# Depthwise and gate steps inside blocks of the second channel product; stores, weight jobs and first loads placed elsewhere

## The chip, the cores and the metric

One core of one Trainium2 chip runs the whole program. The metric is the device time of one execution in microseconds. The kernel before took 1010.52 us (median of 3 runs, 1009.43 to 1011.03).

## The reference, cut to what matters

Three stages follow each other, all in float32; batch B = 4, 12 heads of 64, sequence S = 448, model width 768.

```
attn = sigmoid(q @ k.T / 8 - log S) @ v          # 48 heads, no softmax
x    = attn, heads side by side                  # (4, 448, 768)
h    = (x.T @ U @ V).T ;  u = x + h              # token mixing, rank 32
y    = u + relu(u @ w_ch1) @ w_ch2               # 768 -> 3072 -> 768
gate = sigmoid(causal 5-tap depthwise conv of y over S)
out  = ((y @ w_val) * gate) @ w_out
```

## The kernel before, in words

Activations lie in SBUF transposed (128 channels on the partitions, 448 positions along the row) in one tile `xs`, 6 channel blocks for each of 4 batches. Every float32 product that must be exact is made of three matmuls: an operand is cut into a high part (a copy on ACT that rounds to fp32r) and a low part (a subtraction on DVE), and `mm3` (L438 to L440) adds high x high, high x low and low x high. The large products are also done in Strassen's way, with seven products instead of eight over two batches and two halves of the channels (`seven`, L795). TensorE (PE) therefore needs, for every pair of weight blocks, seven tiles of sums and differences of weights (A11, A12, S2, S1, S3, S4, A22), each with a high and a low half.

**Stages.** `attention_phase` (24 pairs of heads, two per round; the token mixing of batches 0 and 1 lies between its rounds), then `main_phase`: pass p = 0 over batches 0 and 1, pass p = 1 over batches 2 and 3. A pass has six quads q. A quad is two chains of the first channel product (`chain`, 7 x 9 matmuls each, with relu into `hs`) and four blocks of the second (`ch2`, L917: for each of two column halves and two batches 4 x 9 matmuls, then one DVE addition of three PSUM banks into `xs`, L936). So a quad has 270 matmuls in 30 groups of nine. After pass 1 come the value product, the gate and the output product.

**Order.** All engines run hand-placed programs in order. After nearly each group of nine matmuls the program calls `step()`, which takes the next weight job off one list (`pump`, L169), a second one after every eighth step of pass 0 and every fourth of pass 1, and none while the job would bring the live weight tiles over WS = 10. Small parts are put off with `deferred` to the next `flush()`, `later` to the one after. The list is written by `plan()` (L1120): for pass 0 each quad's weights are unpacked from float64 bits, kept in device memory (`keep`) and split; for pass 1 they are read back and split. Each quad of pass 1 lists `pair_jobs` of both chains (6 jobs each), `second_jobs` (4 jobs, or 8 plain loads in quad 0), 3 `gate_jobs` and 13 `form_jobs` for the later value and output weights. Float64 or read-back data come through three `raw` buffers: a load is issued when a buffer's reader is placed (`load_next`).

**Side work.** `sides` maps (pass, quad, event) to units: the token mixing of batches 2 and 3 in pass 0 (transposes, projection, and three `add` units of six small matmuls, L757, that use both banks of `ps_a`), and parked sums `u_sums`. Event 0 comes after the first chain of a quad, event 1 after the second, events 2 to 5 after the four blocks of `ch2`. The last group of a chain (A22, `tail`) is held back and runs after the first group of what follows. In the `ps_a` banks lie also a chain's `y` and `z`; DVE reads them in `both` (L863).

**Queues.** In `main_phase` all transfers are issued by SP in program order: raw loads (L163, L159), kept copies (L196), stash stores and loads (L332, L417), parked tiles (L611). An issue waits in its queue until its data or buffer is ready, and those behind it wait too. `x` tiles have XS = 6 buffers, and a buffer is free again when its kept copy has landed.

**First loads.** `load_kq` (L449) of pair 0: keys (`kq[:, 0]`, 128 rows) on SP, the two halves of the queries (`kq[.., 1]`) on ACT and POOL. `prep_pair` (L480) casts keys on DVE (L490) and queries on ACT (L501), then makes the low parts on DVE (L493), and `scores` (L515) starts.

Of the kernel before, what the change touches and what calls it, by code (L numbers as in the profile page):

```python
# [23 lines left out]
QUAD = 4  # L24
# [23 lines left out]
def tile_kernel(  # L48
# [18 lines left out]
    nc = tc.nc  # L67
# [4 lines left out]
    def later(part):  # L72
        deferred.append(lambda: deferred.append(part))
# [118 lines left out]
    def keep(slot, part, x):  # L192

        if slot not in kept:
            kept[slot] = pools["kept"].tile([P, 2, HQ], F32, tag="kept", name="k_%s%d" % slot)
        side_queue().dma_start(kept[slot][:, part], x)  # L196
# [83 lines left out]
    def second_jobs(p, q):  # L280

        out = []

        def fresh(n, half):
            def job():
                t = wtile(f"w2_{p}_{n}_{half}")
                x = to_x(("w2", n, half))

                def done():
                    forms[p, n, half] = t  # L290
                    keep((f"h{half}_", n // 2), n % 2, x)

                later(lambda: in_two(x, t, done))
            return job

        def again(n, half):
            def job():
                a = loaded.pop(("x", f"h{half}_", n // 2, p))
                ts = [wtile(f"w2_{p}_{n + i}_{half}") for i in range(2)]

                def done(i):
                    forms[p, n + i, half] = ts[i]
                    if i:
                        load_next()

                for i in range(2):
                    in_two(a[:, i], ts[i], lambda i=i: done(i))
            return job

        for half in range(2):  # L310
            kept_already = p or ("w2", QUAD * q, half) in ahead
            for n in range(QUAD * q, QUAD * q + QUAD, 2 if kept_already else 1):
                if kept_already:
                    out.append((2, again(n, half), ("x", f"h{half}_", n // 2, p)))
                else:
                    out.append((1, fresh(n, half), ("w2", n, half)))
        return out
# [131 lines left out]
    def load_kq(p):  # L449

        kq = pools["kq"].tile([P, 2, S], F32, tag="kq", name=f"kq{p}")
        if p == 0:
            nc.sync.dma_start(kq[:, 0], kq_in[p, :, 0])
            for h, queue in enumerate((nc.scalar, nc.gpsimd)):
                queue.dma_start(kq[D * h:D * h + D, 1], kq_in[p, D * h:D * h + D, 1 + h])
        else:
            nc.sync.dma_start(kq[:D], kq_in[p, :D, :2])
            nc.sync.dma_start(kq[D:], kq_in[p, D:, 0::2])
        return kq
# [454 lines left out]
            f"fin{p}_{k}", lambda ws: fetched["out", k, ws, src], f"z{p}", both, last_of, step, before  # L914
        )

    def ch2(p, q, b, half, step, before=None):  # L917
        three = trio(f"ch2_{p}_{q}_{b}_{half}")
        ps = [three[:, j, :S] for j in range(KH)]
        for i in range(QUAD):  # L920
            done_with()
            flush()
            w = weight(p, QUAD * q + i, half)
            if b == halves[p][-1]:
                spent.append(1)
            h = hs[p, QUAD * q + i, b]
            for j in range(KH):
                mm3(ps[j], w, j, h, i == 0, i == QUAD - 1)
            if i < QUAD - 1:
                step()  # L930
            if before and not i:
                before()

        def add():
            y = x_rows(b, half)
            nc.vector.tensor_add(y, three[:, :, :S], y)  # L936

        deferred.append(add)
        step()
# [88 lines left out]
    def attention_phase():  # L1028


        for p, kq in enumerate([load_kq(p) for p in range(2)]):
            load_v(p, kq)
        nc.vector.memset(bias, -math.log(S))
        warm = scratch("warm")[:, :1]
        nc.scalar.activation(warm, bias, AF.Sigmoid)
        nc.gpsimd.memset(xs[:, :, :, :PAD], 0.0)

        zeros = operand("zeros")
        nc.vector.memset(f32(zeros[:, 0]), 0.0)
        idle = pools["ps_s"].tile([P, 2, 512], F32, tag="sc", name="idle")  # L1040
        for _ in range(IDLE):
            mm(idle[:, 0, :S], zeros[:, 0, :P], zeros[:, 0], start=True, stop=True)
        prep_pair(0)
        load_pair(2)
        consts = load_mix()
        steps = prep_mix(*consts)
        side = {(0, 2): steps[:1], (1, 1): steps[1:2], (1, 2): steps[2:]}
        for b in halves[0]:
            units = mix_units(b)
            r = 3 * b + 3  # L1050
            for at, some in (
                ((r, 2), units[:2]),
                ((r + 1, 0), units[2:4]),
                ((r + 1, 2), units[4:5]),
                ((r + 2, 0), units[5:6]),
                ((r + 3, 0) if b == 0 else (r + 2, 2), units[6:]),
            ):
                side[at] = some
        rounds = NP // 2
        todo = [part for k in range(KH) for part in u_sums(0, k)]  # L1060
        def put(at, *parts):
            side[at] = side.get(at, []) + list(parts)

        put((0, 2), *[lambda: load_next(nc.sync)] * RAWS)
        at = iter([(q, k) for q in range(1, rounds) for k in range(3)][2:])
        for key in full_keys + part_keys:
            for part in ahead[key]:
                slot = next(at)
                side[slot] = [part] + side.get(slot, [])
        for slot, n in (((9, 0), 1), ((9, 1), 1), ((9, 2), 2), ((10, 0), 1), ((10, 1), 1), ((10, 2), 2), ((11, 0), 1)):  # L1070
            put(slot, *todo[:n])
            del todo[:n]
        for slot, n in (((10, 1), 1), ((10, 2), 1), ((11, 0), 1), ((11, 1), 2), ((11, 2), 2)):
            put(slot, *[pump] * n)

        def values(p):
            for c in range(NKC):
                attend(p, c)

        def between(q, k):  # L1080
            for step in side.get((q, k), ()):
                step()

        for q in range(rounds):
            p = 2 * q
            for c in range(NKC):
                scores(p, c)
            flush()
            last = q == rounds - 1
            if q:  # L1090
                values(p - 1)
                between(q, 0)
                attend_rest(q - 1)
            else:
                prep_pair(1)
            if not last:
                scores_rest(q)
            flush()
            load_pair(p + 3)
            load_pair(p + 4)  # L1100
            between(q, 1)
            prep_pair(p + 2)
            for c in range(NKC):
                scores(p + 1, c)
            flush()
            values(p)
            between(q, 2)
            prep_pair(p + 3)
        scores_rest(rounds - 1)
        flush()  # L1110
        pump()
        flush()
        values(NP - 1)
        attend_rest(rounds - 1)
# [5 lines left out]
    def plan():  # L1120
# [30 lines left out]
        more = [job for kind in ("val", "out") for k in range(KH) for job in form_jobs(kind, k)]  # L1151
        share = -(-len(more) // (NQ - 1))
        for q in range(NQ):
            for c in (QUAD * q, QUAD * q + 2):
                give(pair_jobs(1, c))
            give(second_jobs(1, q) if q else ready_jobs(1))
            jobs.extend(gate_jobs(halves[0], q))
            give(more[:share])
            del more[:share]

    def main_phase():
# [72 lines left out]
        for p, bs in enumerate(halves):  # L1234
            often[0] = 4 if p else 8
            for q in range(NQ):
                last = q == NQ - 1
                events = iter(range(6))

                def side():  # L1240
                    for unit in sides.pop((p, q, next(events)), ()):
                        unit()

                for i in range(2):
                    if last and i:
                        renew("y" if p else 1)
                    tail = chain(p, QUAD * q + 2 * i, step, tail if i else None)
                    side()
                for half in range(2):
                    for b in bs:  # L1250
                        if last and p and half and b == bs[0]:
                            open_late()
                        ch2(p, q, b, half, step, tail)
                        tail = None
                        if last and p:
                            fetch_next((2, 4, 0, 4)[2 * half + b - bs[0]])
                        side()
                while last and rush:
                    step()
                    flush()  # L1260
# [186 lines left out]
```

## Time and profile before

| | us |
|---|---|
| median of 3 runs | 1010.52 |
| lowest, highest | 1009.43, 1011.03 |
| the profiled execution | 1006.96 |
| its span, first to last instruction | 1005.2 |
| mean granted TensorE clock, share of full | 0.995 |

| engine | busy us | share |
|---|---|---|
| PE matmul | 989.5 | 98% |
| PE weight load | 840.2 | 84% |
| DVE | 736.3 | 73% |
| ACT | 465.5 | 46% |
| POOL | 21.7 | 2% |

Matmuls overlap in the array: one of 448 columns is shown as about 0.37 us, and the next starts about 0.2 us after it. A busy PE therefore says little by itself; the starts of its matmuls and the idle time in brackets say where it stood. In the rows below a line of a timeline is start, duration, engine, line, operation and tiles, and how many like it follow each other (x); the bracket is the idle time of the engine before it, and what ended it.

### The profile page before, as it was taken

The page shows a single profiled execution, that of the slowest core. Times are in us where ns is not written, and L with a number is a line of the kernel's source. Part 1 is how long each engine was busy: PE and PEld are TensorE (multiplying, and loading weights), DVE is VectorE, ACT ScalarE, POOL GpSimd, SP SyncE. Part 2 cuts the span into 40 slices and gives each one's busy share as a digit, 9 for nine tenths or more (in the row PEclk, how much of TensorE's full clock was granted, in tenths as well). Part 3 has the DMA queues.
Part 4 walks back from the last instruction along what each step waited for, and adds up shares of the span by engine and source line. Part 5 has one row for each costly group of instructions (what it writes and reads, how often), then busy time and mean ns, then how long its engine had stood idle before and what let it go on. Part 6 is the DMA issues. An engine that isn't in the chain of part 4 may idle for free.

```text
span 1005.2 us, 14580 instructions
## 1 busy us (share of the span) xinstructions
PE 989.5 (98%) x5208; PEld 840.2 (84%) x5208; DVE 736.3 (73%) x1324; ACT 465.5 (46%) x871; POOL 21.7 (2%) x40
## 2 busy tenths in 40 slices
PE   8999999999999999999999999999999999999998
PEld 4555448988887999998999999998999999999997
DVE  4767797656677787878747979788879777993631
ACT  5767685344353363636333545536354433431331
POOL 0111110000000000000000000000000000000000
PEclk9999999999998999999999999999999999999999
DMA  6967666534546575774835657364546276833745
GB/s 177 273 191 199 164 152 204 169 93 132 141 110 197 172 223 170 221 220 151 313 118 185 221 172 253 118 257 147 210 155 207 98 294 230 282 125 122 258 149 189
DMA packets 83001, 187.52 MB, mean 187 GB/s; under 512 B 14992, under 2 KB 34640, under 8 KB 82928
## 3 DMA queue, kind: packets, MB, share of 16 engines
q1 hardware_dynamic: 79824, 174.64, 55.5%
q0 software_dynamic: 2880, 11.72, 3.9%
q8 instruction: 41, 0.67, 0.3%
q14 instruction: 32, 0.26, 0.1%
q10 hardware_dynamic: 224, 0.23, 0.1%
HBM read 129.14 MB, written 57.41 MB: 186 GB/s over the span
## 4 chain that ended last, share of the span: by engine, by line
PE 62%; DVE 4%; DMA 2%; ACT 1%; issue 1%; SPq 0%; DVEq 0%; ACTq 0%
PE ch L438 9%; PE ch L439 9%; PE ch L440 9%; PE x L438 4%; PE x L440 4%; PE x L439 4%; PE z L438 2%; PE z L440 2%; PE z L439 2%; PE val L439 1%; PE x_fin L439 1%; PE x_fin L440 1%; PE x_fin L438 1%; PE val L440 1%; PE val L438 1%; PE y L438 1%
## 5 line engine op out<-in xcount | busy, mean ns | idle before, releaser
L438 PE MATMUL ch<-h,w 128*128 128x448 f32 x576 | 212.4, 369 | 0.0
L439 PE MATMUL ch<-h,w 128*128 128x448 f32 x576 | 211.7, 368 | 0.2 <-DVE h L858 0.2
L440 PE MATMUL ch<-h,w 128*128 128x448 f32 x576 | 211.5, 367 | 0.0
L438 PEld LDWEIGHTS ch<-h,w 128*128 128x128 f32 x576 | 108.5, 188 | 11.4 <-issue 2.1
L439 PEld LDWEIGHTS ch<-h,w 128*128 128x128 f32 x576 | 108.6, 189 | 10.0 <-DVE h L858 0.8
L440 PEld LDWEIGHTS ch<-h,w 128*128 128x128 f32 x576 | 108.6, 189 | 9.4
L936 DVE TENSOR_TENSOR xs<-ch,xs 128x1344 f32<-128x1344 f32 x48 | 74.7, 1556 | 55.1 <-PE ch L440 55.0
L510 ACT ACTIVATE a<-sc,bias 128x896 f32<-128x896 f32 x72 | 67.3, 1007 | 9.7 <-PE sc L522 9.7
L104 DVE SCALAR_TENSOR_TENSOR x_w<-x_w,r_w 128x384 uint32<-128x384 uint32 x84 | 46.9, 559 | 31.1 <-ACT x_w L100 24.7
L553 PE MATMUL av<-a,vr 128*64 128x448 f32 x288 | 59.4, 548 | 1.3 <-DVE xs L575 1.3
L522 PEld LDWEIGHTS sc<-ks 64*128 64x128 f32 x432 | 38.3, 186 | 23.8 <-ACT a L510 5.1
L522 PE MATMUL sc<-ks 64*128 64x448 f32 x432 | 53.2, 384 | 2.6 <-ACT ks L501 1.2
L100 ACT ACTIVATE x_w<-raw_w 128x384 f32<-128x384 f32 x84 | 45.4, 546 | 19.0 <-DMA k_h<-x_w 8.4
L440 PE MATMUL x<-T,S 128*128 128x448 f32 x144 | 52.9, 368 | 0.5 <-DVE S L203 0.5
L439 PE MATMUL x<-T,S 128*128 128x448 f32 x144 | 52.7, 366 | 0.0
L438 PE MATMUL x<-T,S 128*128 128x448 f32 x144 | 52.7, 366 | 0.0
L553 PEld LDWEIGHTS av<-a,vr 128*64 128x64 f32 x288 | 18.5, 136 | 31.4 <-issue 27.4
L200 ACT ACTIVATE S<-raw_x_w 128x384 fp32r<-128x384 f32 x48 | 23.2, 518 | 38.8 <-DVE raw_x_w L252 12.2
L857 ACT ACTIVATE h<-x 128x448 fp32r<-128x448 f32 x24 | 13.1, 544 | 42.8 <-PE x L440 42.8
L857 ACT ACTIVATE h<-p 128x448 fp32r<-128x448 f32 x48 | 27.5, 573 | 11.3 <-DVE p L863 11.3
L200 ACT ACTIVATE A<-x_w 128x384 fp32r<-128x384 f32 x36 | 18.6, 523 | 27.6 <-PE ch L440 21.9
L200 ACT ACTIVATE S<-x_w 128x384 fp32r<-128x384 f32 x48 | 23.2, 517 | 16.5 <-DVE x_w L260 6.3
(304 smaller groups left out, 2177.5 us busy)
## 6 DMA issues: line engine op xcount, KB each, us to landing
raw_w<-in_w SPq DMA_DIRECT2D x79, 384.0 KB, 3.5
kq<-in_kq SPq DMA_DIRECT2D x47, 224.0 KB, 4.6
raw_x_w<-k_w SPq DMA_DIRECT2D x24, 384.0 KB, 4.5
k_w<-x_w SPq DMA_DIRECT2D x43, 192.0 KB, 3.8
f_val_A<-s_val_A SPq DMA_DIRECT2D x21, 384.0 KB, 3.8
f_out_S<-s_out_S SPq DMA_DIRECT2D x20, 384.0 KB, 3.3
k_h<-x_w SPq DMA_DIRECT2D x36, 192.0 KB, 3.8
raw_w<-in_w POOLq DMA_DIRECT2D x17, 384.0 KB, 4.4
```

The lines of the kernel that those rows point to most:

```text
L100: nc.scalar.activation(f32(x), f32(high), AF.Prelu, scale=2.0 ** -112, alpha=-(2.0 ** 32))
L104: nc.vector.scalar_tensor_tensor(x, x, 3, r, op0=ALU.logical_shift_left, op1=ALU.bitwise_or)
L200: nc.scalar.activation(t[:, 0], x, AF.Copy)
L438: mm(ps, wk[:, 0], x[:, 0], start=start, stop=False, **kw)
L439: mm(ps, wk[:, 0], x[:, 1], start=False, stop=False, **kw)
L440: mm(ps, wk[:, 1], x[:, 0], start=False, stop=stop, **kw)
L510: nc.scalar.activation(a[:, :, :], ps[:, :, :S], AF.Sigmoid, bias=bias, scale=1.0 / math.sqrt(D))
L522: mm(ps[:, h, :S].rearrange("p (c s) -> p c s", c=NSC), ks[r, tk, 0, c], ks[r, tq, 1, :, :SC], start=t == 0, stop=t == 2,)
L553: mm(att["ps"][D * h:D * h + D, :S], vr[:, h, c], a[:, h], start=c == 0, stop=False,)
L857: nc.scalar.activation(t[:, 0], x, AF.Relu)
L936: nc.vector.tensor_add(y, three[:, :, :S], y)
```

## The change

Five edits; the computation stays the same:

1. `second_jobs`: the kept copy of a freshly unpacked block of `w2` is put off by one flush only, instead of being issued with the block's low part two flushes further on.
2. `load_kq`, pair 0: SP and ACT each load one half of the rows, queries first and then keys; POOL issues none.
3. `ch2` has a new argument `inside`, called after its second group of nine matmuls and the step that follows it. `main_phase` passes `side`, so events 1 to 4 lie inside the four blocks of `ch2`; event 0 stays after the first chain, event 5 after the last block. None is left after the second chain.
4. Last round of the attention: `attend_rest` before `between(q, 0)` instead of after it.
5. `plan`, pass 1: the second chain's six jobs and the `second_jobs` are one list `a`; gate and form jobs (16 in quads 0 to 4, 3 in quad 5) are dealt out evenly behind its jobs, instead of all following them.

```diff
-                    keep((f"h{half}_", n // 2), n % 2, x)
-
+
+                deferred.append(lambda: keep((f"h{half}_", n // 2), n % 2, x))
                 later(lambda: in_two(x, t, done))
...
         if p == 0:
-            nc.sync.dma_start(kq[:, 0], kq_in[p, :, 0])
-            for h, queue in enumerate((nc.scalar, nc.gpsimd)):
-                queue.dma_start(kq[D * h:D * h + D, 1], kq_in[p, D * h:D * h + D, 1 + h])
+            for h, queue in enumerate((nc.sync, nc.scalar)):
+                r = slice(D * h, D * h + D)
+                queue.dma_start(kq[r, 1], kq_in[p, r, 1 + h])
+                queue.dma_start(kq[r, 0], kq_in[p, r, 0])
...
             if before and not i:
                 before()
+            if inside and i == 1:
+                inside()
...
                 values(p - 1)
+                if last:
+                    attend_rest(q - 1)
                 between(q, 0)
-                attend_rest(q - 1)
+                if not last:
+                    attend_rest(q - 1)
...
-            for c in (QUAD * q, QUAD * q + 2):
-                give(pair_jobs(1, c))
-            give(second_jobs(1, q) if q else ready_jobs(1))
-            jobs.extend(gate_jobs(halves[0], q))
-            give(more[:share])
+            give(pair_jobs(1, QUAD * q))
+            a = pair_jobs(1, QUAD * q + 2) + (second_jobs(1, q) if q else ready_jobs(1))
+            rest = [(*job, None) for job in gate_jobs(halves[0], q)] + more[:share]
+            n = len(a)
+            for i, job in enumerate(a):
+                give([job] + rest[i * len(rest) // n:(i + 1) * len(rest) // n])
             del more[:share]
...
                     tail = chain(p, QUAD * q + 2 * i, step, tail if i else None)
-                    side()
+                    if not i:
+                        side()
...
-                        ch2(p, q, b, half, step, tail)
+                        ch2(p, q, b, half, step, tail, side)
...
-                        side()
+                side()
```

## Rows read from the trace of the kernel before

**Rows 1.** The page's first part: busy time, share and instructions of each engine.
```profile
PE 989.5 (98%) x5208; PEld 840.2 (84%) x5208; DVE 736.3 (73%) x1324; ACT 465.5 (46%) x871; POOL 21.7 (2%) x40
```

**Rows 2.** Waits of PE: line, releaser, us in total, times, longest.
```profile
PE h L757 <- DVE u L863: 3.2, 2, 2.2
PE x L438 <- DVE p L863: 1.7, 2, 1.1
```

**Rows 3.** Timeline of PE around three `add` units of the mixing.
```profile
238.26 0.46 PE L757 MATMUL h<-vst,pst 32*128 32x448 f32 x1
239.73 0.88 PE L757 MATMUL h<-vst,pst 32*128 32x448 f32 x5 [1.00 <-DVE u L863]
...
303.19 0.47 PE L757 MATMUL h<-vst,pst 32*128 32x448 f32 x1
305.86 1.48 PE L757 MATMUL h<-vst,pst 32*128 32x448 f32 x5 [2.20 <-DVE u L863]
307.27 0.74 PE L438 MATMUL ch<-h,w 128*128 128x448 f32 x1
...
311.92 0.51 PE L438 MATMUL x<-T,A 128*128 128x448 f32 x1
...
318.85 0.87 PE L757 MATMUL h<-vst,pst 32*128 32x448 f32 x6
```

**Rows 4.** Windows: length, busy (count) PE, PEld, DVE, ACT, POOL; PEclk; DMA, GB/s.
```profile
305.40:312.20 6.80, 6.34 (x18) 5.23 (x19) 4.22 (x9) 0.98 (x2) 0.00 (x0) 0.50 0.77 258
```

**Rows 5.** The same view of three stretches of 100 us and one of 204 us.
```profile
350.00:450.00 100.00, 100.00 (x495) 92.67 (x494) 85.12 (x164) 49.41 (x103) 0.00 (x0) 1.00 0.70 208
490.00:590.00 100.00, 100.00 (x485) 90.85 (x484) 68.38 (x116) 40.03 (x80) 0.00 (x0) 1.00 0.55 187
484.50:688.50 204.00, 204.00 (x988) 185.31 (x988) 159.04 (x268) 85.26 (x173) 0.00 (x0) 1.00 0.58 201
700.00:800.00 100.00, 100.00 (x495) 92.63 (x494) 83.23 (x140) 44.63 (x91) 0.00 (x0) 1.00 0.51 172
```

**Rows 6.** Timeline of the first 10 us.
```profile
0.74 0.55 ACTq L455 DMA_DIRECT2D kq<-in_kq  x1
...
1.25 0.65 POOL L455 DMA_DIRECT2D kq<-in_kq  x1 [0.80 <-POOLq L1436]
...
3.58 0.40 DVE L490 CAST ks<-kq 128x448 fp32r<-128x448 f32 x1 [2.22 <-DMA kq<-in_kq]
...
5.67 0.58 ACT L501 ACTIVATE ks<-kq 128x448 fp32r<-128x448 f32 x1 [2.85 <-DMA kq<-in_kq]
...
7.61 2.31 PE L522 MATMUL sc<-ks 64*128 64x448 f32 x14 [0.18 <-DVE ks L506]
```

**Rows 7.** DMA issues of pair 0 on ACT's queue: count, size, us to landing.
```profile
kq<-in_kq ACTq DMA_DIRECT2D x1, 112.0 KB, 3.2
```

**Rows 8.** Timeline at the end of the attention, PE and DVE.
```profile
145.72 2.48 PE L553 MATMUL av<-a,vr 128*64 128x448 f32 x12 [1.27 <-DVE xs L575]
...
153.79 1.15 DVE L575 COPY xs<-av 128x448 f32<-128x448 f32 x2
...
157.46 0.47 PE L440 MATMUL x<-T,S 128*128 128x448 f32 x1 [0.50 <-DVE S L203]
```

**Rows 9.** Timeline of ACT near the end of pass 0.
```profile
463.85 0.55 ACT L100 ACTIVATE x_w<-raw_w 128x384 f32<-128x384 f32 x1 [3.52 <-DMA k_h<-x_w]
```

**Rows 10.** Timeline of DVE in pass 1, quad 3.
```profile
687.54 0.56 DVE L251 TENSOR_TENSOR raw_x_w<-raw_x_w 128x384 f32<-128x384 f32 x1 [2.75 <-DMA raw_x_w<-k_w]
```

**Rows 11.** DMA issues of read-back weights: count, size, median us to landing.
```profile
raw_x_w<-k_w SPq DMA_DIRECT2D x24, 384.0 KB, 4.5
w<-s_w SPq DMA_DIRECT2D x16, 384.0 KB, 4.3
```

**Rows 12.** Costliest groups: one split's high copy on ACT, low part on DVE.
```profile
L203 DVE TENSOR_TENSOR S<-raw_x_w,S 128x384 fp32r<-128x384 f32 x48 | 24.8, 553 | 3.5 <-ACT S L200 3.4
L200 ACT ACTIVATE S<-raw_x_w 128x384 fp32r<-128x384 f32 x48 | 23.2, 518 | 38.8 <-DVE raw_x_w L252 12.2 <-issue 10.4 <-DVE raw_x_w L260 7.1
```

More of the change, by code (lines that the diff above doesn't have):

```diff
@@ L915, in fin_chain, with ch2 @@
         )
-    def ch2(p, q, b, half, step, before=None):
+    def ch2(p, q, b, half, step, before=None, inside=None):
         three = trio(f"ch2_{p}_{q}_{b}_{half}")
```

## The prediction

> **What bounds the kernel now.** I read the engine totals first: PE is busy for 989.5 of 1005.2 us, DVE for 736.3, ACT for 465.5 [rows 1]. The reader is to see there that PE sets the end, and that there is at most some 16 us of idle time to win, plus what lies hidden in slow matmuls. Then the list of PE's waits [rows 2]: in the whole main phase few are over half a microsecond, and four are named by two lines, the mixing's `add` units waiting for DVE (3.2 us in two) and the chains' A22 group waiting for DVE's `p` (1.7 us in two). Then PE's timeline at these places [rows 3], the granted clock there [rows 4], and the count of matmuls in equal stretches [rows 5]. The last shows something that no list of waits shows: with PE never idle and the clock granted in full, 495 matmuls fit into 100 us at 350 and at 700 us, but 485 at 490 us. PE runs at one of two spacings, 202 or 206 ns. The change must therefore be judged by four things: stalls of PE, the clock, the spacing, and new stalls.
>
> **The change part by part.** Times are for the profiled execution, 1006.96 us, which is 3.56 us under the median of the runs; I carry the sum over to the median unchanged.
>
> *Mixing units inside `ch2`.* Before, the `add` unit of event 1 stands right behind the second chain, whose `z` DVE has still to read from the bank that the unit needs. Two of them stall: the first small matmul to the second takes 239.73 - 238.26 = 1.47 us and 305.86 - 303.19 = 2.67 us, while an undisturbed unit issues six in a row [rows 3]. That is 4.1 us. After the second stall the granted clock is half (1.2 instead of 2.4 GHz) until 312.2 us [rows 4]: five small matmuls take 1.48 instead of 0.88 us (0.6 us), and the 12 intervals from 307.27 to 311.92 us take 4.65 instead of 12 x 0.202 = 2.4 us (2.2 us) [rows 3, 5]. Together 6.9 us. Moved, the unit comes 27 matmuls later (first group of the block, A22, second group), 5.5 us at 202 ns, and the longest wait was 2.2 us [rows 2], so the bank is free by then. What is late next: DVE's additions of the unit, which now wait in DVE's queue in the middle of a block; behind them stand weight lows and the relu lows for the next groups, and these had 18 matmuls (3.6 us) in hand. Bounds: 6.9 us gained, or nothing if DVE is late in the new place too; I take 6.9, since 5.5 is more than twice 2.2. The transposes and the parked sums of event 4 come half a block (3.6 us) later; nothing on PE waits for them at once, and I cost them at 0 (at most one more stall like the 1.1 us of [rows 2]).
>
> *First loads.* The query half on POOL is issued at 1.25 and ACT's cast of it starts at 5.67; the keys on SP are there by 3.58. From 5.67 to the steady scores at 7.61 are 1.94 us [rows 6]. The half on ACT's queue landed after 3.2 us [rows 7]. Now the last piece is the second on ACT's queue, issued at 0.74 + 0.55 = 1.29, there at 4.5; with the same 1.94 us behind it scores run at 6.4 instead of 7.6. Gain 1.2 us. From both sides: 1.7 if all pieces are there when ACT's first is (0.74 + 3.2 = 3.94 instead of 5.67), and a loss of 0.4 if the last one needs as long as POOL's half did (4.4 us, so 5.7) and SP's one more issue (0.55 us, as ACT's) delays the next pairs. I take 1.2, the nearest row being ACT's own.
> Against this stands a rule of the Trainium skill (DMA: Bandwidth & Descriptors, Rules for kernel authors): two transfers to disjoint partition halves bring nothing, as both spread over the same engines; one transfer over 128 partitions is to be used. By it this term is 0 and the sum 1.2 us higher. The trace bears on it only by POOL's half being 2 us later than the keys, which tells of the queue, not of the halves.
>
> *End of the attention.* PE waits 1.27 us for DVE's copy of a finished bank, which stood behind `between` [rows 8]. With `attend_rest` first, the copy comes earlier and this wait goes. But DVE has work without a pause from there on; its next copies (153.79) come when they came, and the first chain's second group needs their banks. So PE arrives 1.27 us earlier and waits there; what is left is the later wait of 0.50 us [rows 8], whose chain over ACT starts earlier. Gain 0.5, between 0 and 1.3.
>
> *Kept copies earlier.* ACT waited 3.52 us for a kept copy to land before it could write an `x` tile [rows 9], and DVE's `p` and then PE came late behind it: the smaller of the two A22 waits, 1.7 - 1.1 = 0.6 us [rows 2]. Issued two flushes earlier (about 18 matmuls, 3.6 us) it is no longer late. In SP's queue the copy now waits for DVE's join instead of the later low part; loads behind it wait for no later event than before. Gain 0.6, or 0.
>
> *Weight jobs of pass 1.* I walked both lists through the steps by the code's rule (one job, two at each fourth, none over ten tiles). The 16 jobs dealt out move first chains forward and second products back: the first tiles of a chain in quads 2 to 4 are made 72 to 99 matmuls before their use instead of 18 to 45, and the load that DVE waited 2.75 us for [rows 10] is asked for 72 matmuls ahead instead of 18. That removes the 1.1 us [rows 2]. But the first `w2` tiles of a quad, made 45 to 63 matmuls before use, are now made 27 to 9 before it in quad 0, 9 (1.8 us) in quads 1 to 3 and 18 in quad 4. A read-back takes 4.3 to 4.5 us to land [rows 11], and the split another 0.52 + 0.55 [rows 12], 5.6 us; in quad 3 the load is asked for 27 matmuls (5.5 us) before PE needs it, in quad 0 behind stores that wait for DVE. Behind a late one PE's whole queue stands. Bounds: 0 if the queues run ahead of PE, and 5.6 - 1.8 = 3.8 us in each of five quads, 19 us, if they don't. The nearest row is the late load of [rows 10], which cost PE 1.1 us; I take 1.0 in quad 0, 0.6 in quads 1 to 3, 0.2 in quad 4: 3.0 us lost.
>
> *Spacing.* The slow spacing fills at least the 204 us from 484.5 to 688.5, where PE is never idle (988 matmuls), between the late copy of [rows 9] and the late load of [rows 10]; 204 us x 10/495 = 4.1 us are lost [rows 5]. Both are places that this change touches. Elsewhere the fast spacing held after nearly every disturbance, so I count 4.1 us gained; from both sides, 4.1 gained, or up to 6 lost if most of the time from 500 us on runs slow.
> The Trainium skill (TensorE: Matmul & The Clock Gate, "Wait — 56ns, not 53.3ns?") knows one interval at the full clock, columns by 2.4 GHz and about 2.5 ns, here 189 ns by my estimate. By it there is no such term and the sum is 4.1 us higher. The counts of [rows 5] show two intervals, both longer, and they decide.
>
> Sum: -6.9 - 1.2 - 0.5 - 0.6 - 1.1 + 3.0 - 4.1 = -11.4 us; 995.6 for the profiled execution, 999.1 for the median.
>
> **The rivals.**
> - *Slow spacing stays or spreads.* For it: it held for 204 us at full clock without one idle stretch [rows 5], so one small wait can decide it, and the new late weights are such waits. Against: it is the rarer state. As much of it as before gives 1003.2, most of the time from 500 us on 1009; 1005 for the middle.
> - *The moved units stall as before*, because DVE is late by more than 5.5 us inside the block. Against: 2.2 us was the longest. Without the 6.9 us: 1006.0.
> - *The second product waits for its weights* (slower). Place: the first block of `ch2` in quads 0 to 4 of pass 1. All five late by the full bound cost 19 us instead of 3.0, that is 1015; with half clock after each stall, as after 303 us (2.8 us each, rows 3 and 4), 1029. It decides from a loss of 16.4 us in this place, 3.3 us a quad. For it: a margin of nine matmuls against 5.6 us. Against: the raw loads are asked for ahead, and before the change margins of 18 matmuls mostly passed without a wait of PE.
> - *The halves bring nothing* and the rest holds: 1000.3, inside the forecast's own range.
>
> **How the numbers follow.** Forecast (992 to 1004): 0.63. Spacing: 0.17. Moved units stall: 0.07. Weights late enough to be slower: 0.06. Weights late by 9 to 16 us, 1005 to 1012: 0.07. A difference under 0.2% (2.0 us) can't be told from no change. Faster takes the forecast, most of the spacing rival, the third and half of the last: 0.85. Within 0.2%: 0.08, from the ends of the spacing and late-weight cases. Slower: 0.07. The range 992 to 1008 leaves out about one case in ten above and somewhat fewer below.
>
> **What would show it.** Right: no wait of `h` (L757) for DVE in PE's list, no half clock near 300 us; 495 matmuls in each 100 us of the main phase; steady scores near 6.4 us; no wait of ACT for a kept copy of several us; PE's waits in pass 1 at the first weight of a block, under 1 us each. Wrong: `ch` groups in quads 0 to 4 waiting for ACT's or DVE's `w` by 3 us; counts of 485; the scores still at 7.6 us; a new wait at the y group of the first chain over 1.3 us is expected to stay within the term for the attention's end, and a longer one would refute it.

## The result, and the profile after

The changed kernel is slower: 1015.23 us median of 22 runs (1007.58 to 1021.14) against 1007.61 us for the kernel before in 22 runs (1001.45 to 1013.40). The ratio is 1.0071, 95% interval 1.0053 to 1.0089. Forecast were 999.1 us and a range of 992 to 1008. With more runs the kernel before lies 2.9 us lower than the median that the forecast started from; that is not the error.

The first part of the page of the changed kernel, where [rows 1] showed the kernel before: the same work, the span 11 us longer, PE busy 98% again.
```profile
span 1016.2 us, 14576 instructions
## 1 busy us (share of the span) xinstructions
PE 995.3 (98%) x5208; PEld 843.1 (83%) x5208; DVE 734.3 (72%) x1324; ACT 464.3 (46%) x871; POOL 21.1 (2%) x39
```
PE's waits after (line, releaser, us in total, times, longest), answering [rows 2]:
```profile
PE z L438 <- ACT p L807: 7.8, 3, 3.1
PE ch L438 <- DMA w<-s_w: 4.0, 2, 3.0
...
PE y L438 <- DVE xs L576: 1.0, 1, 1.0
```
The waits of `h` for DVE and of the A22 group for `p` are gone. In their place stand two that the kernel before did not have: the S4 group of a chain (`z`) waits for ACT's copy `p` three times, and the second product (`ch`) waits for weights twice.

PE's timeline at the first of each kind, pass 1, quads 0 and 1:
```profile
522.59 0.37 PE L440 MATMUL z<-B,S 128*128 128x448 f32 x1
525.99 0.71 PE L438 MATMUL ch<-h,w 128*128 128x448 f32 x1 [3.03 <-DMA w<-s_w]
...
568.96 0.36 PE L440 MATMUL x<-T,S 128*128 128x448 f32 x1
572.40 0.47 PE L438 MATMUL z<-B,S 128*128 128x448 f32 x1 [3.08 <-ACT p L807]
```
What ACT and DVE did before 572.40:
```profile
567.41 3.52 DVE L989 SCALAR_TENSOR_TENSOR g<-xs,cw,g 128x896 f32<-128x896 f32 x3
570.85 0.62 DVE L859 SCALAR_TENSOR_TENSOR h<-p,h 128x448 fp32r<-128x448 f32 x1
570.97 0.95 ACT L1005 ACTIVATE g<-g 128x896 f32<-128x896 f32 x1 [3.92 <-DVE g L989]
571.39 0.55 DVE L256 TENSOR_TENSOR raw_x_w<-raw_x_w 128x384 f32<-128x384 f32 x1
571.83 0.53 ACT L807 ACTIVATE p<-z 128x448 f32<-128x448 f32 x1
```
This is the mechanism of the `z` waits in five lines. The gate jobs, dealt out among the chains' weight jobs, leave three depthwise additions of 1.17 us on DVE one after the other. ACT's sigmoid of the gate (L1005) stands at the head of ACT's queue and waits 3.92 us for them. Behind it stands the copy of `z`, which has to be taken before PE's next group adds to the same bank; its data are there at about 567.5 (nine matmuls before the stall), but it runs at 571.83. The same picture returns at 629 and at 690 us, with one or two of the additions just before the sigmoid.

SP's queue before 525.99 (start, duration of the issue, tiles):
```profile
513.07 6.19 SPq L163 DMA_DIRECT2D raw_val<-in_wval  x4
519.93 0.80 SPq L332 DMA_DIRECT2D s_val_A<-A_val  x2
520.77 0.53 SPq L417 DMA_DIRECT2D w<-s_w  x1
```
What SP's queue waited for between 511 and 520.9 us (line, releaser, us in total, times, longest):
```profile
SPq L163 <- DVE r_val L101: 3.0, 2, 1.9
SPq L163 <- DVE S L203: 1.7, 1, 1.7
SPq L163 <- DVE A L203: 1.7, 1, 1.7
...
SPq L332 <- DVE A_val L203: 0.6, 1, 0.6
```
The first split weight of quad 0 is issued at 520.77, which is 21.7 us after the pass begins, and lands 5 us later. Ahead of it stand four raw loads, which waited 6.4 us for DVE to be done with their buffers, and two stash stores of a form job, whose low parts DVE makes.

Three windows (columns as in [rows 4] and [rows 5]):
```profile
350.00:450.00 100.00, 100.00 (x495) 92.67 (x494) 85.07 (x162) 47.77 (x101) 0.00 (x0) 1.00 0.68 203
525.50:528.90 3.40, 2.91 (x8) 2.64 (x9) 0.00 (x0) 0.00 (x0) 0.00 (x0) 0.50 1.00 321
900.00:1000.00 100.00, 100.00 (x486) 90.83 (x485) 47.58 (x83) 26.66 (x53) 0.00 (x0) 1.00 0.55 177
```
Four of the five stalls (all but the shortest, 0.96 us) are followed by 3.4 us at half clock, as the second line shows for the first of them, and behind the last one PE runs at the slow spacing (486 in 100 us) to the end.

Pass 1 begins at 499.1 us instead of 508.6: in these two executions pass 0 and the attention brought 9.5 us. The four quads 0 to 3 of pass 1 then take 61.0, 59.6, 59.3 and 60.4 us; quads 3 to 5 of pass 0, without stalls and at the fast spacing, took 54.7 each.

### The profile page after: what moved, and what is told of

Read it like the earlier page. It is cut to its first block, busy times and chain, and to the rows that moved or that the text cites. A ratio compares the mean times of both kernels' runs of the same rounds, so it can differ in the third digit from the quotient of the medians.

```text
span 1016.2 us, 14576 instructions
## 1 busy us (share of the span) xinstructions
PE 995.3 (98%) x5208; PEld 843.1 (83%) x5208; DVE 734.3 (72%) x1324; ACT 464.3 (46%) x871; POOL 21.1 (2%) x39
## 4 chain that ended last, share of the span: by engine, by line
PE 91%; DVE 5%; DMA 2%; ACT 1%; issue 1%; SPq 0%; DVEq 0%; ACTq 0%
PE ch L438 11%; PE ch L439 11%; PE ch L440 11%; PE x L438 5%; PE x L440 5%; PE x L439 5%; PE av L554 5%; PE sc L523 5%; PE z L438 3%; PE z L440 3%; PE z L439 3%; PE x_fin L438 1%; PE x_fin L440 1%; PE val L439 1%; PE val L438 1%; PE x_fin L439 1%
## 5 line engine op out<-in xcount | busy, mean ns | idle before, releaser
L438 PE MATMUL ch<-h,w 128*128 128x448 f32 x576 | 212.8, 369 | 4.0 <-DMA w<-s_w 4.0
L554 PEld LDWEIGHTS av<-a,vr 128*64 128x64 f32 x288 | 18.5, 136 | 30.0 <-issue 26.7
L200 ACT ACTIVATE A<-raw_x_w 128x384 fp32r<-128x384 f32 x36 | 18.2, 519 | 40.4 <-PE ch L440 37.1
L438 PE MATMUL z<-B,S 128*128 128x448 f32 x72 | 27.5, 382 | 7.8 <-ACT p L807 7.8
L807 ACT ACTIVATE p<-x 128x448 f32<-128x448 f32 x24 | 13.1, 545 | 47.7 <-PE x L440 45.0
```

The source lines that it names most:

```text
L200: nc.scalar.activation(t[:, 0], x, AF.Copy)
L438: mm(ps, wk[:, 0], x[:, 0], start=start, stop=False, **kw)
L554: mm(att["ps"][D * h:D * h + D, :S], vr[:, h, c], a[:, h], start=c == 0, stop=False,)
L807: nc.scalar.activation(t, ps, AF.Copy)
```

## The experiments

Each ratio is against runs of the kernel before on the same chip, with its 95% interval. For the first four kernels that chip ran the kernel before in 1008.42 us (14 runs), for the last four another one ran it in 1005.93 us (21 runs); between the two groups, and with the changed kernel, only ratios can be compared.

**The change without its new list (`no_plan`).**
```diff
-            give(pair_jobs(1, QUAD * q))
-            a = pair_jobs(1, QUAD * q + 2) + ...
+            for c in (QUAD * q, QUAD * q + 2):
+                give(pair_jobs(1, c))
+            give(second_jobs(1, q) if q else ready_jobs(1))
+            jobs.extend(gate_jobs(halves[0], q))
+            give(more[:share])
```


> The change without its new job list of pass 1 (the other four edits stay). Theory (gate jobs): PE's waits of z for ACT's p in quads 1 to 3 of pass 1 (7.8 us in three) and for the w loads of quad 0 (4.0 us in two) are gone, no half clock after 30 us, and the gains of pass 0 stay: the first group of pass 1 starts near 499 us as in the changed kernel, and the time is 7 to 10 us under the kernel before, about 999. Rival (events): the parked sums that come half a block later load DVE at the start of quads 1 to 3 and cause the z waits; then they stay with the old list too, 6 to 8 us, and the time is 1008 to 1012. Rival (spacing): no waits, but counts of 485 matmuls per 100 us over most of the second half, 1003 to 1008.

Measured: 998.20 us, ratio 0.9908 (0.9885 to 0.9931), the lowest ratio of all, clear of the kernel before and of the changed one. Its longest waits of PE in the main phase:
```profile
PE y L438 <- DVE xs L576: 1.0, 1, 1.0
...
PE x L438 <- DVE p L864: 1.0, 2, 0.6
```
No `z` waits, no late loads, no half clock. The events rival is out: the parked sums stand where the changed kernel has them. The profiled execution (998.45 us) had the slow spacing over much of the middle (487 in 100 us at 350) and was fast nevertheless.

**The new list alone (`plan_only`).** The kernel before with the fifth edit only.

> The kernel before with the new job list of pass 1 alone. Theory (gate jobs): the three z waits for ACT's p (6 to 9 us) and the quad 0 waits for w loads (3 to 5 us) are there, each of 2 us and more followed by 3.4 us of half clock (1 to 2 us each); the wait of 1.1 us behind the late load of quad 3 is gone; 12 to 18 us over the kernel before, 1019 to 1026. Rival (events): no z waits, since the parked sums stand where they stood; only the w loads of quad 0 are late, 1009 to 1013.

Measured: 1022.64 us, ratio 1.0138 (1.0105 to 1.0171).
```profile
PE z L438 <- ACT p L806: 7.7, 3, 3.1
PE ch L438 <- DMA w<-s_w: 4.5, 3, 3.1
PE h L757 <- DVE u L863: 3.2, 2, 2.2
```
Both new waits come with the list and nothing else, and the wait behind the late load of quad 3 is gone, as expected. One detail of the expectation failed in this profile: only the stall at 529 us was followed by half clock, the three `z` stalls were not. The profiled execution was also the fastest of the six (1016.86 us, mean granted clock 0.997); four of the others were granted 0.990 to 0.993, so they ran longer at half clock.

**Gate jobs last, form jobs still dealt out (`gates_last`).**
```diff
-            rest = [(*job, None) for job in gate_jobs(halves[0], q)] + more[:share]
+            rest = more[:share]
...
+            jobs.extend(gate_jobs(halves[0], q))
```


> The changed kernel with the 3 gate jobs of a quad behind all its other jobs, as before the change; form jobs stay dealt out. Theory (gate jobs): no z wait for ACT's p in pass 1 over 0.5 us, ACT's sigmoid of the gate waits beside ch2 and costs nothing; the late w loads of quad 0 stay (up to 4 us) unless 3 jobs fewer ahead of them are enough; 1000 to 1006. Rival (events): z waits stay, 6 to 8 us, 1010 to 1015.

Measured: 1003.92 us, ratio 0.9947 (0.9925 to 0.9968).
```profile
PE ch L438 <- DMA w<-s_w: 3.1, 1, 3.1
...
PE z L438 <- ACT p L807: 0.6, 1, 0.6
```
Three jobs per quad, moved back beside the second product, take 7.2 us of `z` waits away. By the ratios the gain over the changed kernel is 12.5 us. An estimate from the two profiles accounts for the rest: the second late load (1.0 us) is gone, and so are the three stretches of 3.4 us at half clock behind the `z` stalls, in which 10 or 11 matmuls ran where 17 fit (some 4 us). The late load stays. In SP's queue it again stands behind raw loads and goes out 22.4 us after the pass begins (501.5):
```profile
515.98 5.95 SPq L163 DMA_DIRECT2D raw_val<-in_wval  x3
523.52 0.33 SPq L159 DMA_DIRECT2D raw_x_w<-k_w  x1
523.90 0.42 SPq L417 DMA_DIRECT2D w<-s_w  x1
```

**The events inside `ch2` alone (`inside_only`).** The kernel before with the third edit only.

> The kernel before with the events inside the blocks of ch2 alone. Theory: the two waits of the mixing's add units for DVE (3.2 us) and the half clock near 305 us are gone; 5 to 7 us under the kernel before, 1000.5 to 1003. Rival (events): z waits for ACT's p appear in quads 1 to 3 of pass 1 and eat the gain, 1007 to 1011.

Measured: 1000.81 us, ratio 0.9933 (0.9911 to 0.9956), that is -6.8 us (-4.4 to -9.0); forecast were -6.9. PE's list has no `h` wait, and no `z` wait either:
```profile
PE x L438 <- DVE p L863: 2.3, 3, 1.0
```

**The sigmoid put off, the list untouched (`late_sigmoid`).**
```diff
-            deferred.append(sigmoid)
+            later(lambda: later(lambda: deferred.append(sigmoid)))
```


> The changed kernel, its job list untouched, with ACT's sigmoid of a gate put off by about three more groups of matmuls. DVE has the same additions at the same places. Theory (order on ACT): the z waits for ACT's p come from the sigmoid that stands in ACT's queue before p and waits for three DVE additions (3.5 us); put off, it finds them done, and the z waits of quads 1 to 3 fall from 7.8 us to under 2 us; the w waits of quad 0 (4 us) stay; 1003 to 1008. Rival (load on DVE): the additions themselves make p, the relu or the weights late; then z, x or ch groups of quads 1 to 3 still wait 5 us or more in all, 1010 to 1015.

Measured: 1009.85 us, ratio 1.0030 (1.0008 to 1.0052). That is above the 1003 to 1008 of the theory; taken from the 1007.61 us against which the changed kernel was measured, the ratio gives 1010.6, inside the rival's range, so the time does not speak for the theory. The waits do: the `z` waits are gone altogether, while DVE has the same additions in the same places; so the order on ACT made them. But other waits came up in quads 1 to 3, 3.9 us in all, and the late loads of quad 0 stayed.
```profile
PE ch L438 <- DMA w<-s_w: 3.4, 2, 2.7
PE ch L438 <- ACT w L200: 2.6, 1, 2.6
...
PE x L438 <- ACT u L807: 0.7, 1, 0.7
PE ch L440 <- DVE w L203: 0.6, 1, 0.6
```
The second line is what the prediction had feared for quads 1 to 3: `w2` made one group ahead and late by 2.6 us in quad 3. ACT's high copy of it waited for the read-back, which SP had issued at 695.96, right behind a stash store (695.54):
```profile
700.58 0.94 ACT L200 ACTIVATE w<-raw_x_h__6_1_7046 128x384 fp32r<-128x384 f32 x2 [2.24 <-DMA raw_x_h__6_1_7046<-k_h]
```
In the changed kernel PE stalls for 2.83 us on `z` before this place, and the wait does not show.

**Quad 0's loads on POOL's queue (`loads_on_pool`),** on top of `gates_last`.
```diff
-                nc.sync.dma_start(f32(t), stash["w2", n, half][:, :, :])
+                (nc.gpsimd if p else nc.sync).dma_start(f32(t), stash["w2", n, half][:, :, :])
```


> The changed kernel with gate jobs last (1003.9 us), and the 8 plain loads of split weights in quad 0 of pass 1 issued by POOL, which has no other work there, instead of SP. Their place in the list stays. Theory (SP's queue): the first w load is late because it stands in SP's queue behind raw loads and stash stores that wait for DVE; on POOL the waits of ch for w loads (3.1 us) and the half clock behind them go, 998 to 1001. Rival (place in the list): the list asks for it too late whatever the queue; waits of 2.5 us or more stay, 1002 to 1005.

Measured: 998.42 us, ratio 0.9923 (0.9899 to 0.9947). The interval overlaps that of `gates_last`, so the ratios alone show no gain over it (taken from 1008.42 us, as `gates_last` was, the ratio gives 1000.7, inside the theory's range). The waits show the cause. No wait of `ch` for a load is left; the longest in the main phase, and the issue of the first load:
```profile
PE ch L439 <- DVE h L859: 1.4, 2, 1.2
```
```profile
512.01 0.54 POOL L417 DMA_DIRECT2D w<-s_w  x1 [358.16 <-DVE u L864]
```
The place in the list is the same as in `gates_last`, but the load goes out 13.2 us after the pass begins (498.8) instead of 22.4, so the queue made it late. With the old list (`no_plan` and the kernel before) it went out after 11.3 us on SP's queue too: it is the issues that the new list puts ahead of it that hold it up.

**Quad 0 listed as before, form jobs dealt out elsewhere, gate jobs last (`best_plan`).**
```diff
+            rest = more[:share] if q else []
...
+            jobs.extend(gate_jobs(halves[0], q))
+            if not q:
+                give(more[:share])
```


> The changed kernel with quad 0 of pass 1 listed as before the change, and in quads 1 to 4 only the form jobs dealt out, gate jobs last. Theory: no waits of ch for w loads, z waits under 1 us in all, no half clock after 30 us; 996 to 1000, and not above the kernel without the new list by more than 2 us. Rival (w2 late): the second product's weights, now one group ahead in quads 1 to 3, make ch groups wait 2 us or more in all; 1001 to 1004. Spacing as found: counts of 495 or 485 per 100 us may move either by 4 us.

Measured: 1000.69 us, ratio 0.9941 (0.9918 to 0.9964): over the expected range, and by the ratios 3.3 us above `no_plan`, where at most 2 were expected. The waits for loads are gone, and the late `ch` groups of the rival did not come; what is left lies mostly in quad 1:
```profile
PE x L440 <- DVE S L203: 1.4, 2, 1.2
PE x L438 <- ACT u L807: 1.3, 2, 1.1
```
So dealing out form jobs shows no gain over the old list: `no_plan` is not beaten. The intervals of the two overlap, and a loss is not shown either.

**The first loads in halves alone (`halves_only`),** one execution.

> The kernel before with the first loads in halves alone; one look for the profile. Forecast: steady scores start 1.2 us earlier than before, near 6.4 us, and the first chain of pass 0 with them. Theory from the changed kernel's trace: only 0.7 us earlier, since the keys' second half on SP lands last (near 5.2 us instead of 4.5). By the rule that halves bring nothing: 0, within 0.2 us.

Measured: steady scores at 7.68 us, against 7.61 in [rows 6]; no gain here. DVE's cast of the keys waits for them until 5.93:
```profile
5.93 0.40 DVE L491 CAST ks<-kq 128x448 fp32r<-128x448 f32 x1 [4.57 <-DMA kq<-in_kq]
```
In the changed kernel the same cast started at 5.26. At 26 us, where the kernels still differ by this edit alone, the scores of the second round start at 26.7 to 27.0 us in the three kernels without it and at 25.3 to 26.8 us in the seven with it, 0.7 us earlier on the mean. From one execution to the next the edit thus brings anything from nothing to 1.4 us: the queries come earlier than from POOL, the keys later than before.

The rule of the Trainium skill (DMA: Bandwidth & Descriptors, Rules for kernel authors), by which transfers to disjoint halves bring nothing, would give 0 here. `halves_only` agrees with it and the mean of the seven does not; as the edit changes queues and order too, no run here tests the halves by themselves.

## Why the prediction was wrong

- *Mixing units, 6.9 us gained: right in the mechanism.* Alone they gave 6.8 (4.4 to 9.0), and the `h` waits and the half clock behind them went. That the two numbers agree to 0.1 is luck: 2.8 of the 6.9 is the half clock of one execution. In three profiles without the edit (`before`, `halves_only`, `plan_only`) quads 1 and 2 of pass 0 take 130.6, 129.3 and 127.8 us, with it (`inside_only`) 123.5: gains of 7.1, 5.8 and 4.3 us.
- *First loads, 1.2 us: mis-sized.* 0.7 on the mean, between 0 and 1.4. In the changed kernel and in `halves_only` the second pieces took 3.5 to 4.6 us to land, not 3.2: the last one came at 5.2 us on SP's queue in the one and at 5.9 on ACT's in the other, not at 4.5.
- *End of the attention, 0.5 us: right in kind.* The wait of 1.27 us went and came back as a wait of `y` for the next copies (1.0 us), as named. Quad 1 of pass 0 starts at 211.3 us in the mean of the six kernels with this edit (210.5 to 212.8, all with the first loads too) and at 212.5 in the four without. Among those that had the fast spacing nearly all the way up to there it is 210.9 in three with both edits against 212.3 in three with neither: 1.4 us for both, forecast were 1.7.
- *Kept copies, 0.6 us: right.* ACT's wait for a kept copy fell from 3.52 [rows 9] to 1.0 us in `no_plan`, and PE's gap there is gone in all kernels with this edit and there in all without it.
- *These four together:* forecast 9.2 us, measured 9.3 (7.0 to 11.6), the ratio of `no_plan`. The mixing units carry most of it; the other three edits together are not resolved by the times.
- *Weight jobs of pass 1, 1.1 gained and 3.0 lost: this step failed.* The 1.1 us were gained, but measured alone the new list costs 13.9 us (10.6 to 17.2) instead of 1.9. I walked the list for weight tiles and raw loads and counted the gate jobs only as places in the list. They are not weight jobs: they carry four DVE additions of about 1.15 us and an ACT sigmoid behind them. Where the old list put them, beside the second product, PE works in banks that DVE frees and needs no copy of a bank by ACT; in the kernel before the same sigmoid waited for DVE too, 11.4 us in six, and no wait of PE came of it (row below, a wait of ACT in the kernel before). In a chain PE needs a copy by ACT one or two groups after its data are there. The prediction asked what is queued behind a late weight, and never what is queued behind the sigmoid. Of the 12 us of listed stalls, 7.8 are these.
```profile
ACT g L1002 <- DVE g L986: 11.4, 6, 2.4
```
- *Quad 0, 1.0 us:* the place was right, and so was the cause in kind (a load held up in SP's queue by issues that wait for DVE, raw loads more than the stores that were named); the size was 4.0, and with half clock behind it more.
- *The rival that was slower* (late second-product weights in five quads) had the right list, but only in quad 0 were these weights late; quads 1 to 3 stalled in their chains, and quad 4 did not stall.
- *Spacing, 4.1 us gained: not settled by the change.* In the changed kernel it was slow from 164 to 212 us, then fast to the first stall, and slow from the last one to the end, 324 us x 9/495 = 5.9 us lost there. In the kernel before it was fast again when it turned slow at 484.5 us, 19 us behind the gap that the late copy made, so the removal of that copy was no reason to count on the fast spacing. It must be taken as a scatter, not as a gain (below).

## What to carry to other kernels

When jobs are dealt out among others, list for each job every instruction it puts on every engine and its wait, and look what the bound engine needs from that engine in the next few microseconds; a wait that was free beside one stage can cost most of its length beside another. A load in an in-order queue is as late as the latest load or store ahead of it, however early it stands in the list. Test such a bundle edit by edit: four of these five were worth 0.9% together and the fifth took it all away.

## What the runs showed of the hardware that was not expected

*Two spacings of the same program.* Six kernels here (the changed one and `no_plan`, `gates_last`, `late_sigmoid`, `loads_on_pool`, `best_plan`) run the same instructions on PE in quads 3 and 4 of pass 0. Between 350 and 450 us, with PE never idle and the clock in full, three of them fit in 495 matmuls and three 486 or 487. Two of the windows, of `no_plan` and of `loads_on_pool`:
```profile
350.00:450.00 100.00, 100.00 (x487) 91.08 (x487) 83.16 (x159) 46.85 (x98) 0.00 (x0) 1.00 0.68 196
```
```profile
350.00:450.00 100.00, 100.00 (x495) 92.67 (x495) 84.36 (x161) 47.54 (x100) 0.00 (x0) 1.00 0.69 202
```
Once set, a spacing holds for tens to hundreds of microseconds. Often it changes at a stall, but not only there: in `no_plan`, `gates_last` and `late_sigmoid` it turned slow near 366 us, in the middle of a block, with no gap between PE's matmuls. Two windows of `no_plan`, before and after that:
```profile
336.00:364.00 28.00, 28.00 (x140) 25.98 (x139) 24.36 (x53) 18.46 (x39) 0.00 (x0) 1.00 0.75 217
368.00:396.00 28.00, 28.00 (x137) 25.45 (x136) 22.38 (x40) 10.13 (x22) 0.00 (x0) 1.00 0.62 185
```
What decides it was not tried and stays open. It is worth up to 2% of a stretch that is bound by PE. It may be part of the scatter of 12 us between runs of one kernel; that is not shown, since timed runs leave no trace. Half clock alone does not make the scatter: five of the six runs of `no_plan` had a mean granted clock of 1.000, and they lie between 996.01 and 1002.05 us.

*The same stall is followed by more or less half clock.* The stall of 2.67 us of [rows 3] was in three executions of the same instructions: the kernel before, `halves_only` and `plan_only`, windows from 303 to 313 us:
```profile
303.00:313.00 10.00, 7.80 (x25) 6.15 (x24) 6.48 (x14) 2.54 (x5) 0.00 (x0) 0.66 0.75 239
```
```profile
303.00:313.00 10.00, 7.80 (x31) 6.27 (x30) 7.12 (x16) 2.83 (x6) 0.00 (x0) 0.83 0.85 251
```
```profile
303.00:313.00 10.00, 7.80 (x38) 6.35 (x38) 7.70 (x16) 4.36 (x9) 0.00 (x0) 1.00 0.81 246
```
The same stall was followed by half clock for 6.8 us, for 3.4 us, and not at all; 25, 31 and 38 matmuls were done. One profile's half clock is therefore one draw of several, and a term that removes it should carry both ends: here 0 to 2.6 us (13 matmuls at 0.2 us).
